# Decode attention on one core: spreading a slab's normalisation, projection and softmax chain over the steps of the next slab

## Chip, core and metric

The kernel runs on one core of one Trainium2 chip. The metric is device time in microseconds (us) of one execution; lower is better. Each version was run several times in alternation with the kernel before on the same chip. Here a run is called slow when it is over 1.5% above the fastest of the same kernel. The span in a profile is about 1.7 us shorter than the time of the same run.

Engine names in the profile: PE is the TensorE matmul, PEld its weight load, DVE is VectorE, ACT is ScalarE, POOL is GpSimd, SP is the engine that issues most loads. PEclk is the granted clock of PE, 1.00 being full speed.

## The reference

Two independent problems, A and B, are computed and their outputs joined. Each is one step of attention decoding over a window of a cache:

```python
# x (2, 1, 576), caches (2, 16, 16384, 128), wq (576, 4096), wo (4096, 576), all bf16
q = (x @ wq).reshape(B, 1, 32, 128)              # 32 query heads
k, v = last W = 4096 positions of each cache     # 16 heads, each used by 2 query heads
p = softmax(q . k * 128**-0.5)
out = (p . v).reshape(B, 1, 4096) @ wo           # (2, 1, 576)
```

K and V are 134 of the 153.1 MB that the kernel moves from HBM; it does little arithmetic on each byte.

## The kernel before

A *slab* is one K/V head of both batch rows: 2 MiB (2.10 MB) of K and as much of V. There are 32 slabs, 16 for each problem. Four slabs make a *group*: they share one score bank in PSUM, one softmax chain, one set of output heads and one 1.18 MB load of wo. A ring of eight slots of 2 MiB holds the K and V slabs, filled by one DMA queue in a fixed order, in which V of slab i comes LAG slabs after K of slab i. A slot is refilled when its last reader is done.

For slab t the work is this, each line on one engine:

```python
make_X(t, jb)   # DVE: transposes half a K slab, ring -> xt           (jb = 0, 1)
make_S(t, jb)   # PE:  8 score matmuls of 512 columns, xt, zq -> st   (jb = 0, 1)
make_Z(t + 4)   # POOL: query operand of a later slab
make_PV(i)      # PE:  64 matmuls of 56 columns, ring (V), pC -> ot   (i = t - LAG)
make_norm(i)    # DVE: ot * rsb -> oTg, 4 columns
```

After the last slab of a group comes the softmax chain. It changes engine at nearly every step:

```python
def make_chain(G):
    # DVE m = max(st); PE transposes it; DVE nM, nMrep; PE broadcasts it; ACT copies it to bias_sb
    # ACT pR = exp(st + bias), twice (w = 0, 1), the first with row sums
    # PE transposes the sums (Ts); DVE pT = transpose(pR), pC = pT * pmask
    # DVE ssum, rs = 1 / ssum; PE broadcasts rs (rsbm); ACT copies it to rsb
    ...
```

and after the PV of a group's last slab its projection: PE spreads `oTg` (rl), DVE masks and sums (`oM`, `oP`), PE multiplies by wo. (The last group has its heads projected one slab at a time.) After problem A's last projection, `make_E` copies the result out of PSUM, half on DVE and half on ACT.

The instructions of each engine run strictly in the order in which this loop adds them, so the loop is the schedule:

```python
LAG = 4
...
for t in range(NSLAB + LAG):
    i = t - LAG
    if t < NSLAB:
        for jb in range(2):
            make_X(t, jb)
            make_S(t, jb)
        if t + 4 < NSLAB:
            make_Z(t + 4)
        if t % 4 == 3:
            make_chain(t // 4)
    if i >= 0:
        make_PV(i)
        make_norm(i)
        G = i // 4
        if contiguous_wo(G):
            if i % 4 == 3:
                make_proj(G)
        else:
            make_proj_direct(i)
        if i % 4 == 3 and (G + 1) % GP == 0:
            make_E(G // GP)
```

## Time and profile before

| | kernel before |
|---|---|
| time, median of 3 | 468.78 us (467.79 to 469.25) |
| span of the profiled run | 465.5 us |
| DVE busy / PE busy | 269.3 us / 287.1 us |
| mean granted PE clock | 0.795 |
| HBM traffic | 329 GB/s over the span |

These lines of the page of the kernel before give the busy time of two engines with its share of the span; the DMA's busy tenths and GB/s in 40 equal slices; the shares of the chain of waits that ended last, by engine and by line; and the two groups of instructions that the change is about (line, engine, operation, output and input, count, then busy us and mean ns of one, then the idle time just before them and what ended it).

```profile
PE 287.1 (62%) x3124; PEld 156.4 (34%) x3124; DVE 269.3 (58%) x206; ACT 19.4 (4%) x50; POOL 30.2 (6%) x144
DMA  8999999999999946999379974499848994897000
GB/s 355 435 412 428 428 427 427 422 430 429 416 370 429 401 183 265 427 429 418 127 306 429 377 315 182 176 424 405 352 190 327 429 423 188 336 394 275 1 0 4
DVE 49%; PE 40%; DMA 6%; issue 3%; ACT 1%; SPq 0%
L416 PE MATMUL st<-xt,zq 128*128 128x512 bf16 x512 | 166.3, 483 | 108.2 <-DVE xt L392 107.6
L522 DVE TENSOR_TENSOR oTg<-ot,rsb 128x4 bf16<-128x4 f32 x32 | 5.2, 162 | 123.0 <-PE ot L507 123.0
```

No engine is full. DVE idles 123.0 us for PV in front of a normalisation that itself takes 0.16 us, and PE idles 108 us for the transposes: the chain of waits goes back and forth between the two. The DMA runs at 427 GB/s for the first third, while the ring still has room, and then in bursts.

The timeline of DVE alone shows one ordinary slab and then the end of a group (start us, duration us, engine, line, operation; in brackets the idle time before it and its releaser).

```profile
142.50 0.16 DVE L522 TENSOR_TENSOR oTg<-ot,rsb 128x4 bf16<-128x4 f32 x1 [3.65 <-PE ot L507]
142.58 7.06 DVE L392 STREAM_TRANSPOSE xt<-ring 128x2048 f32<-128x2048 f32 x2
154.48 0.16 DVE L522 TENSOR_TENSOR oTg<-ot,rsb 128x4 bf16<-128x4 f32 x1 [4.84 <-PE ot L507]
154.56 7.04 DVE L392 STREAM_TRANSPOSE xt<-ring 128x2048 f32<-128x2048 f32 x2
163.94 0.69 DVE L427 TENSOR_REDUCE m<-st 128x1 f32<-128x512 f32 x1 [2.34 <-PE st L416]
...
167.10 1.42 DVE L459 STREAM_TRANSPOSE pT<-pR 128x512 bf16<-128x512 bf16 x2 [1.57 <-ACT pR L451]
...
173.84 0.16 DVE L522 TENSOR_TENSOR oTg<-ot,rsb 128x4 bf16<-128x4 f32 x1 [3.79 <-PE ot L507]
...
175.01 3.59 DVE L392 STREAM_TRANSPOSE xt<-ring 128x2048 f32<-128x2048 f32 x1
```

A slab is 7 us of transposes and then 3.7 to 4.8 us of waiting. At the end of a group the transposes end at 161.6 and start again at 175.0.

One row of the table by stretches of time, for the group between two chain maxima (stretch; its length, busy us and instruction count of PE, PEld, DVE, ACT, POOL; then PEclk, DMA share and GB/s), sums it up: 53.8 us for 33.2 us of DVE work.

```profile
163.90:217.70 53.80, 35.09 (x351) 18.20 (x350) 33.17 (x26) 1.94 (x5) 2.95 (x16) 0.78 0.81 340
```

### The profile page before, as it was taken

How to read it: one execution, taken by the hardware profiler on the slowest of the kernel's cores; microseconds unless marked ns; L12 is line 12 of the kernel's file. 1: busy time of each engine (PE TensorE's matmuls, PEld its weight loads, DVE VectorE, ACT ScalarE, POOL GpSimd, SP SyncE). 2: the span in 40 equal slices, each digit the busy share in tenths (PEclk: the TensorE clock that was granted, in tenths of full speed). 3: DMA queues.
4: the chain of work that ended last, by engine and by line, in shares of the span. 5: the costliest groups of instructions: out<-in, count | busy, mean ns of one | idle time of the engine just before them, and what ended most of it. 6: DMA issues, size and time to landing. Idle time of an engine off the chain costs nothing.

```text
span 465.5 us, 6840 instructions
## 1 busy us (share of the span) xinstructions
PE 287.1 (62%) x3124; PEld 156.4 (34%) x3124; DVE 269.3 (58%) x206; ACT 19.4 (4%) x50; POOL 30.2 (6%) x144
## 2 busy tenths in 40 slices
PE   1556535665866658656555656575586665865667
PEld 1552112331533334222433314232153323422155
DVE  3029966566666636665664662656666663666530
ACT  1000010001000010001000010000100001000010
POOL 5100100000000000000000000000000000000000
PEclk9958977787687877886796785878868777788779
DMA  8999999999999946999379974499848994897000
GB/s 355 435 412 428 428 427 427 422 430 429 416 370 429 401 183 265 427 429 418 127 306 429 377 315 182 176 424 405 352 190 327 429 423 188 336 394 275 1 0 4
DMA packets 11741, 153.54 MB, mean 330 GB/s; under 512 B 1208, under 2 KB 2240, under 8 KB 2368
## 3 DMA queue, kind: packets, MB, share of 16 engines
q1 hardware_dynamic: 11700, 153.10, 79.6%
q8 instruction: 24, 0.39, 0.3%
q14 instruction: 5, 0.04, 0.0%
q10 hardware_dynamic: 12, 0.01, 0.0%
HBM read 153.10 MB, written 0.00 MB: 329 GB/s over the span
## 4 chain that ended last, share of the span: by engine, by line
DVE 49%; PE 40%; DMA 6%; issue 3%; ACT 1%; SPq 0%
DVE xt L392 40%; PE st L416 22%; PE ot L507 14%; DMA ring<-in_A_k_cache_dram 6%; DVE pT L459 2%; DVE pC L473 2%; PE pj L571 1%; DVE m L427 1%; DVE oTg L522 1%; PE tb L482 1%; ACT pR L451 1%; PE tb L437 1%; PE tb L551 1%; PE pj L539 1%; DVE nM L430 0%
## 5 line engine op out<-in xcount | busy, mean ns | idle before, releaser
L392 DVE STREAM_TRANSPOSE xt<-ring 128x2048 f32<-128x2048 f32 x64 | 225.0, 3592 | 21.2 <-DMA ring<-in_A_k_cache_dram 21.2
L416 PE MATMUL st<-xt,zq 128*128 128x512 bf16 x512 | 166.3, 483 | 108.2 <-DVE xt L392 107.6
L416 PEld LDWEIGHTS st<-xt,zq 128*128 128x128 bf16 x512 | 53.0, 114 | 212.1 <-DVE xt L392 138.0
L522 DVE TENSOR_TENSOR oTg<-ot,rsb 128x4 bf16<-128x4 f32 x32 | 5.2, 162 | 123.0 <-PE ot L507 123.0
L507 PEld LDWEIGHTS ot<-pC,ring 128*128 128x128 bf16 x2048 | 66.2, 102 | 6.7 <-issue 1.6
L507 PE MATMUL ot<-pC,ring 128*128 128x56 bf16 x2048 | 68.0, 196 | 0.0
L378 POOL TENSOR_TENSOR zq<-qs,bmask 128x16 bf16<-128x16 bf16 x128 | 23.5, 216 | 355.6 <-PE st L416 341.7
L571 PE MATMUL pj<-wob,oP 128*2 128x288 bf16 x112 | 24.1, 396 | 4.9 <-DVE oP L563 4.9
L459 DVE STREAM_TRANSPOSE pT<-pR 128x512 bf16<-128x512 bf16 x16 | 11.4, 712 | 12.6 <-ACT pR L451 12.6
L482 PE MATMUL tb<-rs,ones_f 1*128 1x16 f32 x16 | 4.8, 379 | 21.5 <-DVE rs L481 21.5
L254 PE MATMUL tb<-xU,ring 128*128 128x56 bf16 x288 | 12.5, 219 | 8.0 <-DMA ring<-in_B_wq_dram 5.8
L571 PEld LDWEIGHTS pj<-wob,oP 128*2 128x2 bf16 x112 | 11.8, 110 | 14.6 <-DVE oP L563 5.6
L427 DVE TENSOR_REDUCE m<-st 128x1 f32<-128x512 f32 x8 | 5.5, 691 | 19.3 <-PE st L416 19.3
L440 ACT ACTIVATE bias_sb<-tb 128x1 f32<-128x1 f32 x8 | 1.4, 171 | 364.1 <-PE tb L437 364.1
L254 PEld LDWEIGHTS tb<-xU,ring 128*128 128x128 bf16 x288 | 12.3, 119 | 8.2 <-DMA ring<-in_B_wq_dram 5.9
L451 ACT ACTIVATE pR<-st,bias_sb 128x512 bf16<-128x512 f32 x16 | 12.7, 818 | 0.3
L482 PEld LDWEIGHTS tb<-rs,ones_f 1*128 1x128 f32 x16 | 4.0, 305 | 23.3 <-DVE rs L481 23.3
L473 DVE TENSOR_SCALAR pC<-pT,pmask 128x256 bf16<-128x256 bf16 x32 | 8.4, 335 | 0.3
L236 PE MATMUL tb<-ident_b,xt 2*128 2x2 bf16 x36 | 2.3, 194 | 9.8 <-DVE xt L204 9.8
L455 PE MATMUL tb<-ident_f,rsum 128*1 128x128 f32 x8 | 2.5, 308 | 9.3 <-ACT pR L451 9.3
L437 PE MATMUL tb<-ones_f,nMrep 1*128 1x1 f32 x16 | 3.0, 256 | 4.9 <-DVE nMrep L434 4.9
L428 PE MATMUL tb<-ident_f,m 128*1 128x128 f32 x8 | 2.2, 270 | 6.3 <-DVE m L427 6.3
(42 smaller groups left out, 46.3 us busy)
## 6 DMA issues: line engine op xcount, KB each, us to landing
ring<-in_A_k_cache_dram SPq DMA_DIRECT2D x16, 2048.0 KB, 20.7
ring<-in_A_v_cache_dram SPq DMA_DIRECT2D x16, 2048.0 KB, 12.7
ring<-in_B_k_cache_dram SPq DMA_DIRECT2D x16, 2048.0 KB, 9.4
ring<-in_B_v_cache_dram SPq DMA_DIRECT2D x15, 2048.0 KB, 9.9
ring<-in_A_wq_dram SPq DMA_DIRECT2D x1, 4608.0 KB, 13.5
ring<-in_B_wq_dram SPq DMA_DIRECT2D x1, 4608.0 KB, 25.4
wob<-in_A_wo_dram SPq DMA_DIRECT2D x4, 1152.0 KB, 15.5
wob<-in_B_wo_dram SPq DMA_DIRECT2D x4, 1152.0 KB, 10.4
```

The source lines that it names most:

```text
L254: last = e.matmul(bank[:, c * 64:c * 64 + NS], wqv[P][:, u, cb * 128:(cb + 1) * 128], xU[:, P, u, 0:NS], start=(u == 0), stop=(u == NU - 1))
L378: last = e.tensor_tensor(dst, src, msk, ALU.mult)
L392: Xop[(t, jb)] = S.add("dve", lambda e: e.transpose(xt[:, n % NXT, :].bitcast(FP32).rearrange("p (c b r) -> p c r b", b=Bb, r=16), ring[:, ...
L416: last = e.matmul(st[:, 0:512], zq[:, p4, m, b, 16 - 16 * jb:144 - 16 * jb], mv, start=first, stop=True, skip_group_check=True)
L427: mx = S.add("dve", lambda e: e.tensor_reduce(m1[:], st[:, :], AX.X, ALU.max), [Sop[(4 * G + 3, 1)]] + prev("Tm"), "max%d" % G)
L451: return e.activation(dst, st[:, :].rearrange("p (q x r) -> p q x r", x=2, r=16), ACTF.Exp, bias=bias_sb[:, 0:1], scale=SCALE, **({"accum_ ...
L459: chain[(G, "pT%d" % w)] = S.add("dve", lambda e, w=w: e.transpose(pT[:, w, :], pR[:, w, :]), [exs[w]] + prev("pC"), "pT%d_%d" % (G, w))
L473: last = e.tensor_scalar(dst, src, pmask[:, b:b + 1], None, ALU.mult)
L482: n4, b4, rb = tb_job(lambda e, bank: e.matmul(bank[:, 0:16], ones_f[0:1, 0:128], rs[0:1, 0:16], start=True, stop=True), "rsbm%d" % G, [ch ...
L507: last = e.matmul(ot[:, 0:NS], ring[:, r, j * 128:(j + 1) * 128], pC[:, v, col:col + NS], start=(j == 0), stop=(j == KR - 1))
L522: norm_op[i] = S.add("dve", lambda e: e.tensor_tensor(oTg[:, v, 2 * m:2 * m + 2, :], OT[i % 2][:, 0:4].rearrange("d (b h) -> d h b", h=2), ...
L571: last = e.matmul(PJ[half][0:Bb, 0:NH], oP[:, v, j, :], wob[:, v, j, half * NH:(half + 1) * NH], start=(proj_start(G) and j == 0), stop=Tr ...
```

## The change

The intent is to have something for DVE to do while PE works on PV and while the chain hops between engines. Nothing is computed differently. The normalisation of slab i-1, and the spread of its projection, move into the next step, behind that slab's first transpose; the multiplication by wo moves to the end of that step. The chain is cut in three and laid around the second transpose of the next group's first slab. V follows K by 5 slabs, so that the group's PV starts one step later.

```diff
-    LAG = 4
+    LAG = 5
 ...
-        for t in range(NSLAB + LAG):
+        for t in range(NSLAB + LAG + 1):
             i = t - LAG
             if t < NSLAB:
-                for jb in range(2):
-                    make_X(t, jb)
-                    make_S(t, jb)
+                make_X(t, 0)
+                make_S(t, 0)
+            Gc = t // 4 - 1 if t % 4 == 0 and 4 <= t <= NSLAB else None
+            if Gc is not None:
+                make_chain(Gc)              # maximum .. exp
+            Gp = (i - 1) // 4 if i >= 1 and (i - 1) % 4 == 3 else None
+            if i >= 1:
+                make_norm(i - 1)
+                if not contiguous_wo((i - 1) // 4):
+                    make_proj_direct(i - 1)
+                elif Gp is not None:
+                    make_spread(Gp)         # rl, oM, oP
+            if t < NSLAB:
+                make_X(t, 1)
+                make_S(t, 1)
                 if t + 4 < NSLAB:
                     make_Z(t + 4)
-                if t % 4 == 3:
-                    make_chain(t // 4)
-            if i >= 0:
+            if Gc is not None:
+                make_chain2(Gc)             # Ts, pT, pC, ssum, rs
+            if 0 <= i < NSLAB:
                 make_PV(i)
-                make_norm(i)
-                ...projection and copy of the result, here
+            if Gc is not None:
+                make_chain3(Gc)             # rsbm, rsb
+            if Gp is not None:
+                if contiguous_wo(Gp):
+                    make_proj(Gp)           # only the multiplication by wo
+                if (Gp + 1) % GP == 0:
+                    make_E(Gp // GP)
```

(The bodies of the chain and of the projection are only cut into these functions.)

More of the change, by code (lines that the diff above doesn't have):

```diff
@@ L424, in make_chain @@
             st = ST[G % 2]
-            v = G % 2
             prev = lambda k: [chain[(G - 1, k)]] if G >= 1 else []
@@ L454, in make_chain, with make_chain2 @@
             exp_op[G] = exs[1]
+            chain[(G, "exps")] = exs
+        def make_chain2(G):
+            v = G % 2
+            prev = lambda k: [chain[(G - 1, k)]] if G >= 1 else []
+            exs = chain[(G, "exps")]
             n3, b3, ts = tb_job(lambda e, bank: e.transpose(bank[0:1, 0:128], rsum[:, 0:1], ident_f[:]), "Ts%d" % G, [exs[0], p_ident_f])
@@ L481, in make_chain, with make_chain3 @@
             chain[(G, "rs")] = S.add("dve", lambda e: e.reciprocal(rs[0:1, 0:16], ssum[0:1, 0:16]), [sm] + prev("rsbm"), "rs%d" % G)
+        def make_chain3(G):
+            v = G % 2
             n4, b4, rb = tb_job(lambda e, bank: e.matmul(bank[:, 0:16], ones_f[0:1, 0:128], rs[0:1, 0:16], start=True, stop=True),
@@ L542, in make_proj_direct, with make_spread @@
             proj_op[G] = S.add("pe", f, [norm_op[i], stream_dma[("W", G)]], "projd%d" % i)
-        def make_proj(G):
-            P = G // GP
+        def make_spread(G):
             v = G % 2
@@ L565, in make_proj @@
                 [mo] + ([proj_op[G - 2]] if G >= 2 else []), "oP%d" % G)
+        def make_proj(G):
+            P = G // GP
+            v = G % 2
             def f(e):
@@ L589, in build_kernel @@
             make_Z(t)
-        for t in range(NSLAB + LAG):
+        for t in range(NSLAB + LAG + 1):
             i = t - LAG
             if t < NSLAB:
-                for jb in range(2):
-                    make_X(t, jb)
-                    make_S(t, jb)
+                make_X(t, 0)
[13 more added lines that the diff above has]
+                make_S(t, 1)
                 if t + 4 < NSLAB:
                     make_Z(t + 4)
-                if t % 4 == 3:
-                    make_chain(t // 4)
-            if i >= 0:
+            if Gc is not None:
+                make_chain2(Gc)
+            if 0 <= i < NSLAB:
                 make_PV(i)
-                make_norm(i)
-                G = i // 4
-                if contiguous_wo(G):
-                    if i % 4 == 3:
-                        make_proj(G)
-                else:
-                    make_proj_direct(i)
-                if i % 4 == 3 and (G + 1) % GP == 0:
-                    make_E(G // GP)
+            if Gc is not None:
[5 more added lines that the diff above has]
+                    make_E(Gp // GP)
         S.check()
```

## The prediction

> **What bounds it now.** The span is 465.5 us and no engine is full: PE 62%, VectorE 58%, DMA about 80% (busy shares, DMA queues). The chain of waits alternates: VectorE 49%, PE 40%; mainly K transposes (40%), score matmuls (22%), PV (14%). The timeline shows why. VectorE runs a slab's two transposes (3.52 us each), then the normalisation, which waits for that slab's second scores (1.9 us) and PV (1.67 us): 123 us over 32 slabs (the waits view). PE meanwhile waits 108 us for transposes. An ordinary slab takes 10.8 to 12 us. Each fourth adds the softmax chain, during which no slab work is done (last score 163.9, next transpose 175.0). A group of four takes 53.7 to 58.5 us; VectorE is busy 33.1 of them.
>
> DMA is second: 427 GB/s while slots are free, 305 to 340 once the ring is full (windows by group). 153.1 MB at 428 GB/s is 358 us.
>
> **What the change does.** No arithmetic or bytes removed. The normalisation of slab i-1 follows the next slab's first transpose (3.52 us), about as long as scores plus PV (3.6 us warm): 0 to 0.3 us of the wait remain. The maximum overlaps the next first transpose, the exponentials the second; the group's PV starts a step later, which LAG 5 allows. Slots are still released four steps ahead.
>
> **Costs per group of four, estimated from those durations:**
> - two ordinary slabs: 7.04 + 0.16 + 0.3: 7.5 each;
> - chain slab: 7.0 + 4.2 (maximum 0.70, nM 0.28, nMrep 0.21, pT 1.43, pC 1.05, sum, reciprocal 0.5) + about 2 for the transposed maximum, which stands behind the next first scores on PE: 13 to 14.5;
> - spread slab: 7.0 + 0.16 + 0.6 + 2.3 for the spread matmuls behind the scores: 10.2; then projection (2.1 warm, 4.0 cold) delays PE and the next norm by 1.5 to 4.
>
> Sum 39 to 44, against 54 to 58. PE idles 3 to 4.4 us in the chain and spread slabs. The Trainium skill, "TensorE: Matmul & The Clock Gate", Part 1, says the clock halves after an idle window of about 3.4 us; this trace agrees: after 3.76 us idle, eight score matmuls take 3.37 us (granted clock 0.50 to 0.55), not 1.9. I expect one or two cold stretches per group, not one per slab, and take 41.5.
>
> DMA per group: 16.8 MB + 1.18 MB of wo, 42 us at 428 GB/s. The two limits nearly meet.
>
> **The sum.** Compute: first four slabs end at 59.3 as now; seven groups of 41.5, less 3 (PV not yet started): last transpose ends at 347; tail (last chain, five PVs, projections, output) 25, now 26; a wait for problem A's output copy 5: 377. DMA floor: 360 plus 5 for the last PV piece, projection, output: 365. Measured times lie about 3 above the span: **379 us**, range **368 to 400**. Chances: faster by over 2% 0.97, within 2% 0.02, slower 0.01.
>
> **What would show it right.** VectorE's wait for PV falls from 123 us to under 35; VectorE stays near 269 us busy, over 70% of the span; DMA holds about 425 GB/s up to about 360 us; nM's wait for the transposed maximum (now 2.9 us in total) becomes 10 to 25, oM's for the spread matmuls (now 3.3) too; the mean score matmul falls below 483 ns.
>
> **What would make it wrong.** Below 368 is barred by DMA. If PE is cold in most slabs (scores 3.4 each, PV 3.1: 10 us a slab), groups take 46 and the time passes 400. If the wo load, which waits for a now later projection, blocks the DMA stream, gaps show in the DMA row.

## The result

| | before | after |
|---|---|---|
| time, median of 4 | 468.87 us (467.79 to 469.25) | 372.86 us (370.98 to 373.24) |
| span of the profiled run | 465.5 us | 370.9 us |
| DVE busy / idle | 269.3 / 196.2 us | 266.0 / 104.9 us |
| mean granted PE clock | 0.795 | 0.867 |
| HBM traffic over the span | 329 GB/s | 413 GB/s |

The ratio of the times is 0.7947, with a 95% interval of 0.7917 to 0.7977: 20.5% less. (A ratio here is the mean time of one kernel's fast runs over that of the other's of the same rounds, so not quite the ratio of the medians quoted.) The result is correct. The second run of the same kernel in the experiments gave 371.11 us.

The page of the changed kernel, the same lines as before:

```profile
PE 247.6 (67%) x3124; PEld 145.8 (39%) x3124; DVE 266.0 (72%) x206; ACT 19.5 (5%) x50; POOL 30.3 (8%) x144
DMA  8999999999999999999999999999999999999991
GB/s 323 441 415 426 426 422 434 429 426 433 419 428 426 431 419 429 429 426 426 427 425 428 428 424 430 426 429 426 423 429 426 429 420 429 427 424 373 433 417 78
PE 48%; DVE 40%; DMA 8%; issue 2%; SPq 0%; ACT 0%
L416 PE MATMUL st<-xt,zq 128*128 128x512 bf16 x512 | 148.3, 440 | 94.6 <-DVE xt L392 81.0
L530 DVE TENSOR_TENSOR oTg<-ot,rsb 128x4 bf16<-128x4 f32 x32 | 4.8, 148 | 24.3 <-PE ot L515 23.4
```

The normalisation's wait for PV fell from 123.0 to 23.4 us. Of these, 10.2 us are in the tail, after the last transpose. The DMA now streams without a gap at its full rate. The one dip, 373 GB/s in the fourth slice from the end, is where the last wo load waited for an earlier projection.

DVE's timeline through the last two slabs of a group, then the slab with the chain (first transpose up to 223, second at 225.99), then the slab with the spread:

```profile
208.83 0.16 DVE L530 TENSOR_TENSOR oTg<-ot,rsb 128x4 bf16<-128x4 f32 x1 [2.43 <-PE ot L515]
208.90 7.12 DVE L392 STREAM_TRANSPOSE xt<-ring 128x2048 f32<-128x2048 f32 x2
216.18 0.16 DVE L530 TENSOR_TENSOR oTg<-ot,rsb 128x4 bf16<-128x4 f32 x1
216.25 7.10 DVE L392 STREAM_TRANSPOSE xt<-ring 128x2048 f32<-128x2048 f32 x2
223.21 0.63 DVE L426 TENSOR_REDUCE m<-st 128x1 f32<-128x512 f32 x1
225.46 0.28 DVE L429 TENSOR_REDUCE nM<-tb 1x16 f32<-1x128 f32 x1 [1.62 <-PE tb L427]
...
225.99 3.62 DVE L392 STREAM_TRANSPOSE xt<-ring 128x2048 f32<-128x2048 f32 x1
229.47 1.24 DVE L464 STREAM_TRANSPOSE pT<-pR 128x512 bf16<-128x512 bf16 x2
...
233.50 0.28 DVE L482 TENSOR_REDUCE ssum<-tb 1x16 f32<-1x128 f32 x1 [1.71 <-PE tb L460]
...
233.99 3.58 DVE L392 STREAM_TRANSPOSE xt<-ring 128x2048 f32<-128x2048 f32 x1
...
239.76 0.29 DVE L562 TENSOR_TENSOR oM<-tb,hmask 128x128 f32<-128x128 f32 x1 [2.18 <-PE tb L558]
```

An ordinary slab is now 7.3 us (208.90 to 216.18), with no wait at all at 216.18. What waits are left stand at the chain (1.62 and 1.71 us), at the spread (2.18), and once for the PV of the spread's slab (2.43), whose second scores ran at half clock.

The group's row in the table by stretches:

```profile
182.30:223.20 40.90, 29.47 (x355) 17.13 (x352) 32.66 (x26) 1.95 (x5) 2.96 (x16) 0.83 1.01 426
```

So this group takes 40.9 us instead of 53.8, with the same DVE work (32.7 against 33.2 us). Over the whole run DVE's idle time fell by 91.3 us and its busy time by 3.3 us, and these two are the 94.6 us of span. The PV wait alone fell by 99.6 us, more than the whole. The chain's, spread's and output copy's waits did not shrink in sum. They were 42.9 us before (maximum 19.3, pT 12.6, output copy 4.8, oM 3.3, nM 2.9) and are 50.5 us after (oM 15.1, nM 12.4, ssum 10.8, output copy 8.7, maximum 2.0, pT 1.5). PE's granted clock rose too, from 0.795 to 0.867, and could pass for a rival cause. For the PV wait it is the smaller part. Before, no wait in the loop's 21 slabs without a chain was under 3.65 us, and this is the wait with PE at full clock (second scores 1.91 us, PV 1.67); only 8.5 of their 85.1 us come on top. In the seven slabs with a chain PV itself ran at half clock (3.04 to 3.11 us instead of 1.67), about 10 us in all. So, by this estimate, the slow clock explains about 19 of the 123.0 us.

The larger part of what follows asks which half of the change did what, and what stops the kernel now.

### The profile page after: what moved, and what is told of

Same layout as the page of the kernel before. It is cut to its first block, busy times and chain, and to the rows that moved or that the text cites. A ratio compares the mean times of both kernels' runs of the same rounds, so it can differ in the third digit from the quotient of the medians.

```text
span 370.9 us, 6834 instructions
## 1 busy us (share of the span) xinstructions
PE 247.6 (67%) x3124; PEld 145.8 (39%) x3124; DVE 266.0 (72%) x206; ACT 19.5 (5%) x50; POOL 30.3 (8%) x144
## 4 chain that ended last, share of the span: by engine, by line
PE 48%; DVE 40%; DMA 8%; issue 2%; SPq 0%; ACT 0%
DVE xt L392 36%; PE st L416 31%; PE ot L515 12%; DMA ring<-in_A_k_cache_dram 8%; PE pj L582 4%; DVE oTg L530 1%; PE pj L547 1%; DVE nM L429 1%; DVE ssum L482 1%; DVE rs L486 1%; DVE oM L562 0%; DVE nMrep L433 0%; PE tb L558 0%; PE tb L460 0%; DVE pT L464 0%
## 5 line engine op out<-in xcount | busy, mean ns | idle before, releaser
L416 PE MATMUL st<-xt,zq 128*128 128x512 bf16 x512 | 148.3, 440 | 94.6 <-DVE xt L392 81.0
L416 PEld LDWEIGHTS st<-xt,zq 128*128 128x128 bf16 x512 | 49.2, 106 | 172.4 <-DVE xt L392 93.8
L515 PEld LDWEIGHTS ot<-pC,ring 128*128 128x128 bf16 x2048 | 64.0, 100 | 9.7 <-issue 5.7
L515 PE MATMUL ot<-pC,ring 128*128 128x56 bf16 x2048 | 64.5, 193 | 0.0
L530 DVE TENSOR_TENSOR oTg<-ot,rsb 128x4 bf16<-128x4 f32 x32 | 4.8, 148 | 24.3 <-PE ot L515 23.4
L582 PE MATMUL pj<-wob,oP 128*2 128x288 bf16 x112 | 14.8, 286 | 0.0
L562 DVE TENSOR_TENSOR oM<-tb,hmask 128x128 f32<-128x128 f32 x7 | 2.0, 291 | 15.1 <-PE tb L558 15.1
L429 DVE TENSOR_REDUCE nM<-tb 1x16 f32<-1x128 f32 x8 | 2.2, 278 | 12.4 <-PE tb L427 12.4
L582 PEld LDWEIGHTS pj<-wob,oP 128*2 128x2 bf16 x112 | 8.8, 83 | 4.1
L482 DVE TENSOR_REDUCE ssum<-tb 1x16 f32<-1x128 f32 x8 | 2.2, 278 | 10.8 <-PE tb L460 10.8
```

What stands on the lines that cost most here:

```text
L416: last = e.matmul(st[:, 0:512], zq[:, p4, m, b, 16 - 16 * jb:144 - 16 * jb], mv, start=first, stop=True, skip_group_check=True)
L429: nm = S.add("dve", lambda e: e.tensor_reduce(nM[0:1, 0:16].rearrange("o (p h) -> o p h", p=8), b1[0:1, 0:128].rearrange("o (a p h) -> o p ...
L482: sm = S.add("dve", lambda e: e.tensor_reduce(ssum[0:1, 0:16].rearrange("o (p h) -> o p h", p=8), b3[0:1, 0:128].rearrange("o (a p h) -> o ...
L515: last = e.matmul(ot[:, 0:NS], ring[:, r, j * 128:(j + 1) * 128], pC[:, v, col:col + NS], start=(j == 0), stop=(j == KR - 1))
L530: norm_op[i] = S.add("dve", lambda e: e.tensor_tensor(oTg[:, v, 2 * m:2 * m + 2, :], OT[i % 2][:, 0:4].rearrange("d (b h) -> d h b", h=2), ...
L582: last = e.matmul(PJ[half][0:Bb, 0:NH], oP[:, v, j, :], wob[:, v, j, half * NH:(half + 1) * NH], start=(proj_start(G) and j == 0), stop=Tr ...
```

## The experiments

Theory: the larger loss was the wait of each normalisation for its own PV, the smaller one the chain; the lag matters little; and the changed kernel stops at two limits that nearly meet, its engines at about 41 us a group and the DMA at about 42. Rivals: the chain was the main loss; both parts are needed together; the lag feeds the DMA better; or only one of the two limits counts. A count of "us a group" below is the distance between two chain maxima on DVE.

### Only the normalisation and projection moved

The changed loop, but with the chain in one piece at the end of each fourth slab, and lag 4:

```diff
-    LAG = 5
+    LAG = 4
-            if Gc is not None: make_chain(Gc)      # and chain2, chain3 below
+                if t % 4 == 3:                     # behind make_Z
+                    make_chain(t // 4); make_chain2(t // 4); make_chain3(t // 4)
```

> Only the normalisation, the spread and the projection move into the next slab's steps; the softmax chain stays one lump at the end of every fourth slab, V follows K by 4. Theory (the wait of VectorE for PV was the larger loss, the chain lump the smaller): ordinary slabs fall from 10.8-12 us to 7.3-7.6 us, the lump keeps its gap of 8 to 10 us on VectorE, a group takes 43 to 46 us, time 385 to 400 us, that is about four fifths of the whole gain of 96 us. VectorE's wait for PV falls below 40 us. Rival (both parts are needed, since an early normalisation only moves the wait into the lump): time above 420 us.

Measured: 387.83 us (385.37 to 389.67), ratio to before 0.8287. Groups took 41.6 to 43.8 us, the first 37.0 and the one with problem A's output copy 49.5. The normalisation's wait for PV is 28.0 us in total:

```profile
DVE oTg L530 <- PE ot L515: 28.0, 22, 4.1
```

(DVE's line 530 waited for PE's line 515: us in total, times, longest.) So this half alone takes off 80.6 us (468.45 to 387.83). The theory's range holds; the rival that both are needed falls. The edit moves the normalisation and the projection together, so what each is worth by itself was not taken apart.

### Only the chain spread

The changed kernel with the normalisation and the whole projection behind their own PV, as before:

```diff
-            if i >= 1:
-                make_norm(i - 1) ...               # and the spread
+            if 0 <= i < NSLAB:                     # behind PV and chain3
+                make_norm(i) ...                   # spread, projection and copy as in the kernel before
```

> Only the softmax chain is spread over the next slab's steps, V follows K by 5; normalisation and projection stay right behind their own PV. Theory: ordinary slabs keep 10.8 to 12 us, the chain's slab falls to about 17 us, a group takes 49 to 52 us, time 430 to 445 us, so 25 to 40 us of the 96. VectorE's wait for PV stays above 110 us. Rival (the chain lump is the main loss): time below 410 us.

Measured: 441.85 us (441.39 to 442.41), ratio 0.9436, so 26.6 us less than before. Groups took 51.2 to 51.7 us, except the first and last (47.6, 47.7) and the one with the output copy (54.7).

```profile
DVE oTg L530 <- PE ot L515: 104.3, 32, 4.8
```

The wait for PV is nearly all still there. I had written "above 110 us", which is a miss by 6 us; the time and the groups are as expected. The chain was the smaller loss. The two halves give 80.6 and 26.6 us alone, 107 together, but only 96 us when both are in. A part is counted twice: the wait for PV fell by 95.0 us in the one and by 18.7 us in the other, but by only 99.6 us in both together.

### Only the lag

The kernel before with one number changed, `LAG = 5`.

> The kernel before with the lag of V behind K set to 5, order of work unchanged. Theory: the lag alone buys nothing, groups stay at 54 to 58 us, and the tail has one PV without a transpose beside it more; the first group has one PV less: time 464 to 474 us. Rival (the ring with a longer lag feeds the DMA better and is part of the gain): below 460 us.

Measured: 462.30 us (461.19 to 466.59), ratio 0.9889, interval 0.9837 to 0.9942. This lies just under the theory's range and above the rival's, so the theory was a little off: the lag does buy something in the old order, 1.1%. The first group has one PV less and took 44.6 us instead of 48.7. And the projection no longer falls right behind the chain, where PE's clock was down (0.52 granted from 121.2 to 125.0 us; five of the seven projections took 3.9 to 4.0 us, the other two 2.12). The two pages show the projection's matmuls, first of the kernel before:

```profile
L571 PE MATMUL pj<-wob,oP 128*2 128x288 bf16 x112 | 24.1, 396 | 4.9 <-DVE oP L563 4.9
```

and with lag 5 alone:

```profile
L571 PE MATMUL pj<-wob,oP 128*2 128x288 bf16 x112 | 14.8, 286 | 4.9 <-DVE oP L563 4.9
```

The same 112 matmuls take 9.3 us less. The tail was 2.7 us longer. The rival's mechanism, better feeding of the DMA, does not show: the span moved 333 GB/s against 329, as the shorter time makes it.

### The changed kernel with lag 4

One number in the changed kernel, `LAG = 4`.

> The changed kernel with the lag set back to 4. Theory: the chain's values are ready before PV asks for them even then (pT and pC end 2.3 us after the second transpose, the scores before PV take 1.9 to 3.6 us), so the lag of 5 is not needed; the spread falls into the chain's slab, and two waits of VectorE (for the transposed maximum and for the spread matmuls) merge into one; groups 38 to 40 us, less than the changed kernel's 41, and the DMA floor of about 366 us of span binds: time 366 to 373 us. Rival (the lag is what makes the spreading possible): PV waits for pC in each chain slab, groups over 43 us, time over 385 us.

Measured: 372.69 us (371.74 to 374.02), ratio 0.7961. The same time as the changed kernel, and correct, so the lag of 5 is not what makes the spreading possible. But the reason for the time is another one. With lag 4 the spread falls into the chain's slab and its wait shrinks (oM 4.8 us instead of 15.1), DVE gets ahead of the loads, and it now waits for K, in 12 places after the first K:

```profile
DVE xt L392 <- DMA ring<-in_A_k_cache_dram: 29.5, 5, 22.2
DVE xt L392 <- DMA ring<-in_B_k_cache_dram: 14.9, 8, 2.7
```

The changed kernel waits for K only once, for the first:

```profile
DVE xt L392 <- DMA ring<-in_A_k_cache_dram: 20.8, 1, 20.8
```

In the chain of waits of this run DMA has 51%, in the changed kernel 8%. Groups became 42 us on average ((309.42 - 98.06) / 5 = 42.3): the DMA's pace, not the 38 to 40 us that I expected. With the DMA as the limit the theory's 38 to 40 could not be seen.

### Half the V bytes

The V loads (but for the last) fetch half of each slab, and PV runs its 64 matmuls on the half that is there. The result is wrong (relative error 0.72); no engine's work changes. By the page 120.6 MB are read instead of 153.1, so 32.5 MB are gone (31 in MiB).

```diff
-ring[:, r, :]                          <- V slab, 64 blocks
+ring[:, r, 0:SW // 2]                  <- V slab, blocks 0 to 31
-ring[:, r, j * 128:(j + 1) * 128]      # PV's operand
+ring[:, r, (j % 32) * 128:(j % 32 + 1) * 128]
```

> The changed kernel with the V loads cut to half of each slab's bytes (all but the last V); PV runs the same 64 matmuls on the half that is there, so the result is wrong on purpose and no engine's work changes. 31 MB of the 153 are gone. Theory (engines bind the changed kernel's loop, the DMA only nearly does): no transpose waited for K before, so groups stay at 39 to 41 us and the time at 369 to 373 us. Rival (the DMA binds): the time falls by 10 us or more, toward 300 us.

Measured: 373.56 us median of 4, but 377.81, 373.59 and 373.54 were slow against a single fast run of 367.86, which lies under the theory's range, and the profile was of a slow one. The same kernel ran again with more rounds:

> The kernel with half the V bytes once more, because three of its four runs before were marked slow against a single fast one. Theory (engines bind the changed kernel): runs spread over 366 to 378 us as PE's clock falls, none under 364 us, though 31 MB less are loaded. Rival (the DMA binds, and the one run at 367.86 us was the true state): most runs at 368 us or below.

Measured: six runs, 367.60, 367.81, 372.63, 372.86 (fast), 373.67, 373.85 (slow), ratio of the fast ones 0.7921. They fall into two clusters that go with PE's mean granted clock: 0.883 to 0.888 at 367.6 to 367.8, 0.867 to 0.872 at 372.6 to 373.9. The changed kernel has the same two: in its second set of runs, below, 370.90 to 371.11 at 0.884 to 0.898 and 372.87 to 373.53 at 0.871. All six lie in the theory's 366 to 378 us; the rival wanted most of them at 368 us or below, and two are. Taking 32.5 MB away, which is 76 us of the DMA at 427 GB/s, therefore saves about 3 us in the first cluster and nothing that shows in the second. (The two kernels ran on different chips, on which the kernel before differed by 1.2 us, 467.77 and 468.97, so these differences are good to about 1 us.) So engines bind the loop of the changed kernel, and in its better clock state the DMA stands right behind them. The first profile of this kernel (the run of 377.81 us) shows that the DMA's row is full of gaps again, while DVE is as busy as with all bytes (266.1 us against 266.0):

```profile
DVE  3106998898777898488887797628976896787530
DMA  8999999999975799937994699856987599603930
```

### Half the transposes

The opposite test: each transpose of K takes half the columns, and the score matmuls read them twice, so PE's work is unchanged.

```diff
-ring[:, r, jb * HW_:(jb + 1) * HW_]  -> xt[:, n % NXT, :]
+ring[:, r, jb * HW_:jb * HW_ + HW_ // 2] -> xt[:, n % NXT, 0:HW_ // 2]
-[[partition], [128, 32], [2, 16]]     # score operand
+[[partition], [0, 2], [128, 16], [2, 16]]
```

> The changed kernel with each transpose of K cut to half its columns; the score matmuls read those twice, so PE's work is the same; wrong result on purpose. VectorE loses about 14 us of its 33 per group. Theory (the DMA stands right behind the engines): groups take 42 us, the time of 17.96 MB at 427 GB/s, VectorE waits for K loads, and the time stays at 367 to 373 us. Rival (only the engines bind, with room below): time falls toward 320 us.

Measured: 370.86 us (370.67 to 370.91), ratio 0.7925. DVE is busy 158.5 us instead of 266.0, and the time does not move: DVE waits for K instead.

```profile
DVE xt L392 <- DMA ring<-in_A_k_cache_dram: 71.7, 13, 20.8
DVE xt L392 <- DMA ring<-in_B_k_cache_dram: 64.2, 11, 6.1
```

So the theory holds: behind the engines stands the DMA, at 370.9 us. This run passed the comparison with the reference, though half the scores came from the wrong keys. So with these inputs the comparison does not catch wrong scores.

### Fewer waits

The first version takes away DVE's 8 us wait in front of problem A's output copy, by adding the copy one slab later:

```diff
-                if (Gp + 1) % GP == 0:
-                    make_E(Gp // GP)
+            while late:
+                make_E(late.pop())
+            if Gp is not None and (Gp + 1) % GP == 0:
+                late.append(Gp // GP)
```

The second also puts the transposed maximum ahead of the next first scores on PE, and `oM` and `oP` behind the second transpose:

```diff
             if t < NSLAB:
                 make_X(t, 0)
+            if Gc is not None:
+                make_max(Gc)          # maximum and its transpose
+            if t < NSLAB:
                 make_S(t, 0)
 ...
                 make_S(t, 1)
+            if Gp is not None and contiguous_wo(Gp):
+                make_spread2(Gp)      # oM, oP
```

The changed kernel ran beside them on the same chip.

> The changed kernel again, unaltered, as the measure for the two runs beside it: 371 to 374 us.

> The changed kernel with problem A's output copy one slab later, where its projection is long done. Theory (engines bind by less than 2 us): the 8 us wait of VectorE goes, but the last V bytes land at about 365 us whatever the engines do, and 4 to 5 us of PV, normalisation, projection, copy and output follow: 370 to 373 us, a gain of 0 to 2 us on the changed kernel. Rival (the engines bind alone): a gain of 6 to 8 us.

> The changed kernel with all three waits taken out (transposed maximum ahead of the next first scores, oM and oP after the second transpose, output copy later), full loads. Theory: engines would take 34 to 36 us a group, the DMA 42, so VectorE now waits for K loads in every group and the time stops at the DMA's floor: 369 to 372 us. Rival (engines bind alone): under 350 us.

Measured: the changed kernel 371.11 us (370.90 to 373.53), ratio 0.7939; the later copy 370.89 us (370.68 to 371.06), ratio 0.7917; all three waits out 370.94 us (370.85 to 371.18), ratio 0.7920. The intervals of the ratios overlap: none of the three is shown faster. What the edits do take away is the slower cluster of runs, as no run of the two came out above 371.2 us. In the version with all waits out, DVE waits for K again, here for problem B's (for A's three times, 8.7 us in all, after the first):

```profile
DVE xt L392 <- DMA ring<-in_B_k_cache_dram: 33.2, 12, 3.2
```

To see what the edits are worth to the engines, the same version ran with half the V bytes (wrong result):

(In the text below, "there" means the chain's and the spread's slab.)

> Three waits taken out of the changed kernel (the transposed maximum goes ahead of the next first scores on PE; oM and oP come after the second transpose instead of waiting for the spread matmuls; problem A's output copy comes one slab later) and, to see what that is worth without the DMA in the way, the V loads cut to half their bytes (wrong result on purpose). Theory: VectorE loses 1.6 + 1.7 + 2.2 us of waits a group and 8 us once, [...]second scores there take 1.9 instead of 3.6 us and the next normalisation's wait of 2.4 us goes too: groups 34 to 36 us, time 325 to 340 us. Rival (PE's cold stretches do not hang on these gaps, and only VectorE's own waits go): second scores stay at 3.6 us, groups 36 to 38.5 us, time 341 to 360 us.

Measured: 325.14 us (321.81 to 326.56), ratio 0.6938. Groups took 33.6 us on average ((298.19 - 96.49) / 6), the mean granted clock was 0.93 to 0.94. The time lies at the lower end of the theory's range, the groups slightly below theirs. One part of the theory is only half right. In the spread's slab the second scores are now at full clock ("warm": 1.91 us after 1.40 us idle), but in two of the groups its first scores are at half clock ("cold": 3.51 and 3.59 us). In the chain's slab the second scores follow the same gap each time, about 2.2 us behind a small matmul, and yet PE's timeline in this run shows them now warm, now cold:

```profile
168.44 1.90 PE L421 MATMUL st<-xt,zq 128*128 128x512 bf16 x8 [2.20 <-DVE xt L397]
...
201.91 3.51 PE L421 MATMUL st<-xt,zq 128*128 128x512 bf16 x8 [2.21 <-DVE xt L397]
```

Of seven such places three took 1.90 us, two about 3.5 us and two lay between (2.53 and 2.68 us). The Trainium skill, "TensorE: Matmul & The Clock Gate", Part 1, says that the clock's window runs freely and does not start anew with the kernel. The traces agree: in all thirteen, the moments at which the granted clock changes are whole multiples of 3.413 us apart. They also show what the clock goes by here, if PE's busy time is read step by step on this grid (from 65 us on). In this run it fell after each of the 6 full-clock steps in which PE was busy for 1.36 us or less, and stayed up after each of the 59 with 1.49 us or more; in the kernel before it fell after all 29 with 1.29 us or less and stayed up after all 35 with 1.83 us or more. (In some other traces the two kinds of step overlap between 1.4 and 1.9 us.) So it fits that the same gap is warm or cold by where it lies on the grid. This may be what makes the two clusters of run times; that last step was not tested.

In this run DVE waits for K only once, for the first:

```profile
DVE xt L397 <- DMA ring<-in_A_k_cache_dram: 21.0, 1, 21.0
```

So with all waits out the DMA hides 45.8 us (370.94 to 325.14) of what the engines could save. This is not where the missing 11 us of the two halves went: with half the V bytes the changed kernel itself gained at most about 3 us. Three versions that differ in their engine work or order (half the transposes, later copy, all waits out) all stop at 370.9 us with these loads.

## Why the prediction was right

Predicted 379.0 us, 368 to 400; measured 372.86 us. Point by point:

- *The alternation of DVE and PE is the main loss, the chain the smaller one.* Shown: 80.6 us for the one half alone, 26.6 us for the other. But the lag of 5, which the prediction named as what allows the later PV, was not needed: 372.69 us with 4.
- *"0 to 0.3 us of the wait remain".* Shown for ordinary slabs: no wait at 216.18. In total 23.4 us, under the 35 foretold. What is left in the loop, 13.2 us, stands mostly after the spread's slab (2.43 us in the group shown), where cold second scores of 3.60 us come before PV. The prediction put this wait (1.5 to 4 us) down to the projection's load on PE; the next normalisation, which does come behind the projection, did not wait.
- *Ordinary slabs 7.5 us, chain slab 13 to 14.5, spread slab 10.2.* Measured in one group: 7.3 us, 14.2 us (first transpose from about 219.8, the next slab's at 233.99) and 9.9 us.
- *41.5 us a group.* Measured 40.9 to 41.0 in three groups in the middle, 38.0 to 39.7 in three others, and 46.8 in the one with the output copy.
- *nM's and oM's waits 10 to 25 us each; score matmul under 483 ns; DVE over 70% busy.* Measured 12.4 and 15.1 us, 440 ns, 72%. Not foreseen was a third wait of this kind, for the transposed sums (ssum, 10.8 us).
- *The output copy of problem A 5 us.* Measured 8.0 us. But the last transpose ended at 347.0 us with that wait included, where the sum had 347 without it, because the groups without it took 39.8 us on average ((349.00 - 62.28 - 8.0) / 7), not 41.1 (41.5, the first 3 less). So two errors offset each other, the groups 8.8 us too long in sum and the copy 3 us too short, and the number owes that much to luck. The last transpose is 5 us of the 6 by which 379 was too high, and the tail was 23.9 us, not 25.
- *One or two cold stretches a group.* The prediction drew on the Trainium skill, "TensorE: Matmul & The Clock Gate", Part 1, which puts the idle window that halves the clock at about 3.4 us. The trace of the changed kernel agrees in the spread's slab: after 4.21 us idle, eight score matmuls take 3.60 us, against 1.91 us after 1.93 us idle. In the chain's slab the scores are as cold after only 3.24 us (3.59 us at 229.66), so a group in the middle has two cold stretches, as foretold; but the length of the gap alone is not the measure (see "Fewer waits").

```profile
202.98 3.60 PE L416 MATMUL st<-xt,zq 128*128 128x512 bf16 x8 [4.21 <-DVE xt L392]
...
219.91 1.91 PE L416 MATMUL st<-xt,zq 128*128 128x512 bf16 x8 [1.93 <-DVE xt L392]
```

- *"The two limits nearly meet."* Shown: half the V bytes save at most about 3 us, half the transposes save nothing, and the version with fewer waits is bound by loads. The DMA streams at 427 GB/s with this core running alone: the Trainium skill, "HBM Reference", "Specifications (TRN2)", says that a core streaming alone measures about 425 GB/s and two cores of a pair about 358 GB/s each. This agrees with the first; no run here shows the second.
- *"DMA floor: 360 plus 5."* This term was mis-sized. The floor is 369.2 us of span (the run with all waits out), since the stream does not stop sharply. The table by stretches of that run gives, for the end of its loads (GB/s is the last column):

```profile
358.00:360.00 2.00, 0.59 (x4) 0.19 (x4) 0.00 (x0) 0.00 (x0) 0.00 (x0) 1.00 0.97 408
360.00:361.00 1.00, 0.26 (x10) 0.27 (x11) 0.00 (x0) 0.00 (x0) 0.00 (x0) 1.00 0.67 279
362.00:363.00 1.00, 0.75 (x24) 0.59 (x21) 0.16 (x1) 0.00 (x0) 0.00 (x0) 1.00 0.56 238
364.00:365.00 1.00, 0.61 (x24) 0.61 (x24) 0.00 (x0) 0.00 (x0) 0.00 (x0) 1.00 0.36 147
365.00:366.00 1.00, 1.00 (x46) 1.00 (x42) 0.00 (x0) 0.00 (x0) 0.00 (x0) 1.00 0.00 0
```

  The last bytes land between 364 and 365 us, not at 360, and 4 to 5 us of PV, projection and output follow. The DMA share (last but one) falls with the rate, from 0.97 to 0.36, which fits engines that have run out of bytes better than slower engines; why they end apart was not tried. In this kernel the lower bound of the prediction, 368 us, was therefore out of reach by about 3 us.
- *The wo load might block the stream.* It waited 57.3 us in total for projections, but the queue was deep enough: one slice of forty dipped to 373 GB/s.

## What to carry to other kernels

When two engines each idle about as long as the other works, put one piece of independent work between a producer and its consumer in the program order of each engine; here one 3.5 us transpose between PV and its normalisation, with the projection moved along, was worth four fifths of the gain. Then look for the next limit before polishing: an experiment that takes bytes away and one that takes engine work away tell which of them binds. Here they showed that 46 us of further engine savings would be hidden by the loads. Set a DMA floor by when the last bytes land, not by bytes over rate alone.

## What the Trainium skill lacked or had wrong

- "TensorE: Matmul & The Clock Gate", Part 1: the page speaks of an idle window of about 3.4 us. Here a shorter gap was followed by cold matmuls in some cases: 3.51 us for eight score matmuls after 2.21 us idle behind a small matmul (1.90 us is warm, and the same gap gave that too). How much work a window may hold and still count as idle is not said there: here the clock fell after 3.41 us steps with up to 1.36 us (that run) or 1.29 us (the kernel before) of PE busy.
- "DMA: Bandwidth & Descriptors", Bandwidth: nothing is said there of how a long stream ends. Here its rate fell from 408 to 279, 238 and 147 GB/s over the last 5 us, and the last bytes land some 6 us later than bytes over rate (153.1 MB at 427 GB/s is 358.5 us), the slower start included.
